# The first layer's 128x256 tile products of five units written as seven block products each, with the work order remade behind them

## The chip, the cores and the metric

The kernel runs on one core of a Trainium2 chip. The metric is device time in microseconds (us) of that core; the median of three runs of the kernel before is 290.37 us (290.33 to 292.88).

## The reference

Two stages follow each other. The first is attention with a mask by hashing: queries and keys of 4 batches, 8 heads, 768 positions and 64 dimensions are projected on six directions, the six signs make a bucket, and a query sees only keys of its own bucket. The second is a two-layer network over the joined heads (512 columns): layer norm, 512 to 2048 columns, relu, back to 512, and the sum with its input.

```
q_bits = (einsum('bhsd,dk->bhsk', q, proj) > 0);  k_bits likewise
mask   = q_bucket[:, :, :, None] == k_bucket[:, :, None, :]
attn   = softmax(where(mask, q @ k.T / sqrt(64), -1e9))
x      = (attn @ v), heads joined            # 4 x 768 x 512
xn     = (x - mean) / sqrt(var + 1e-6) * g_ln
out    = x + relu(xn @ w_ch1) @ w_ch2        # w_ch1: 512 x 2048, w_ch2: 2048 x 512
```

## The kernel before, in words

The work is cut into twelve **units** of 256 query rows, three for each batch, numbered 0 to 11. A unit has two head groups g of four heads. For each unit and group the scores are made in six steps of 128 keys (`S_`, into PSUM tiles `sc`), `E_` takes the exponential on ScalarE (tiles `E`, 128x1024), and `A_` multiplies by the values into the accumulator `acc`. `na` and `nb` normalise into `x`, `nc_` and `ag` make the layer norm's statistics, `ce` the centred and scaled rows `xc`, and `fl` transposes them by a DMA into `xnT`.

The network's first layer is `F_`: eight words per unit, each with eight matmuls of 128 rows of `w_ch1` by 256 moving columns, into a PSUM bank `f`; `R_` (ScalarE or VectorE) takes the relu into `hb`. The second layer of units 1 to 11 is already done by seven block products (`P_`) with sums of `hb` blocks (`ss`) on VectorE and `Y_` adding each product to `x`. `O_` stores.

PSUM is handed out by tag: the tag `pp` has three slots of two banks each (scores and `acc`), the tag `f` has two slots of one bank (everything of the network, and small products). SBUF tiles of many kinds share fifteen slots of tag `E`.

Nothing in the program is scheduled at run time: the string `ORDER` is a list of words like `F.t.7.3` (function, engine, unit, part). The program walks the list and issues each word's instructions to its engine, so each engine's queue is its words in the list's order, and semaphores make an engine wait for what it reads and for slots to come free. `SLOTS` says which slot each tile gets. `WIDE` and `SUMS` are switches; `WIDE` is empty before.

The functions of the seven first-layer products (`w1s`, `bs`, `M_`, `V_`, `U_`, `Q_`, `ru`) stand in the file before as well, but no word of the list before calls them. Their scheme for one unit: `w1s` makes sums of blocks of `w_ch1` (eight instructions for the whole kernel, kept in slots that the loads of queries and keys used, two in `E` slots), `bs` makes four sums of blocks of `xnT`, and `M_` does the seven products in two halves h of 512 hidden columns, each word 8 matmuls with 128 moving columns. Their sums stand in three PSUM tiles per half: `Ma` (products 1, 6, 7, 4), `Mb` (product 2) and `Me` (products 5, 3). `V_` copies a stage of such a sum to SBUF (after products 1, 6 and 5), `U_` adds a PSUM sum and a copy into `hb`, `Q_` takes the relu of the last stage of `Ma`, and `ru` takes the relu of the three blocks that `U_` wrote.

Of the kernel before, what the change touches and what calls it, by code (L numbers as in the profile page):

```python
# [65 lines left out]
tu.v.2.1.0.1 S.t.5.0.0 N.a.5.0.0 S.t.5.0.1 E.a.5.0.0.1 S.t.5.0.2 P.t.2.2 Y.v.2.2 E.a.5.0.0.0 E.a.5.0.0.2  # L66
nb.v.4.0 fl.s.3.1 F.t.3.6 R.v.3.6 ss.v.2.2 P.t.2.1 Y.v.2.1 cv.v.2.0.2 S.t.4.1.3 S.t.4.1.4 N.a.4.1.1 S.t.4.1.5
# [9 lines left out]
R.v.3.1 mr.s.2.1.0 S.t.5.1.3 N.a.5.1.1 S.t.5.1.4 E.a.5.1.1.1 S.t.5.1.5 E.a.5.1.1.2 nb.v.5.0 P.t.3.2 ss.v.3.1
Y.v.3.2 P.t.3.1 P.t.3.5 S.t.6.0.0 E.a.5.1.1.0 CA.v.3.0.1 N.a.6.0.0 mr.s.2.1.1 lv.s.3.0.2 S.t.6.0.1 S.t.6.0.2
E.a.6.0.0.0 E.a.6.0.0.2 ss.v.3.2 Y.v.3.1 ss.v.3.4 Y.v.3.5 P.t.3.6 P.t.3.3 ss.v.3.3 nc.v.5.0 A.t.5.1.0.1
A.t.5.1.0.2 tu.v.3.0.0.2 A.t.5.1.0.0 Y.v.3.6 A.t.5.1.1.0 A.t.5.1.1.2 A.t.5.1.1.1 mr.s.2.1.2 na.v.5.1  # L80
E.a.6.0.0.1 fl.s.4.0 lv.s.2.4.3 P.t.3.7 tu.v.3.0.0.0 Y.v.3.3 nb.v.5.1 O.s.2.3 S.t.6.0.3 N.a.6.0.1 S.t.6.0.4
S.t.6.0.5 CA.a.3.0.0 Y.v.3.7 hm.t.3.0 bt.v.3.0 P.t.3.4 Y.v.3.4 lv.s.3.0.3 F.t.4.6 E.a.6.0.1.0 O.s.2.1
E.a.6.0.1.2 E.a.6.0.1.1 lv.s.3.0.1 nc.v.5.1 ag.v.5.1 ag.v.5.0 R.a.4.6 F.t.4.0 S.t.6.1.0 S.t.6.1.1 N.a.6.1.0
rs.p.5 S.t.6.1.2 R.v.4.0 ce.v.5.0 cv.a.2.4.2 F.t.4.7 E.a.6.1.0.0 cv.v.2.4.0 F.t.4.4 R.a.4.7 ce.v.5.1 on.p.2
fl.s.5.0 A.t.6.0.1.0 A.t.6.0.0.2 tu.v.3.1.0.1 E.a.6.1.0.1 E.a.6.1.0.2 A.t.6.0.1.2 lv.s.3.0.0 R.v.4.4 sp.t.2.0
A.t.6.0.0.1 sc.v.2.0 A.t.6.0.1.1 su.v.2.4 A.t.6.0.0.0 F.t.4.5 F.t.4.2 fl.s.5.1 R.a.4.5 na.v.6.0 nb.v.6.0
F.t.4.1 R.v.4.1 S.t.6.1.3 mw.s.3.0 S.t.6.1.4 N.a.6.1.1 S.t.6.1.5 R.a.4.2 E.a.6.1.1.1 P.t.4.2 O.s.3.0
lv.s.3.4.0 lv.s.3.4.3 tu.v.3.1.0.0 Y.v.4.2 E.a.6.1.1.2 F.t.4.3 tu.v.3.1.1.0 tu.v.3.1.1.2 R.a.4.3 tu.v.3.1.1.1
cv.v.3.0.0 ss.v.4.1 O.s.3.2 F.t.5.3 R.a.5.3 F.t.5.2 R.v.5.2 tu.v.3.1.1.3 E.a.6.1.1.0 P.t.4.1 Y.v.4.1 ss.v.4.2
ss.v.4.4 S.t.7.0.0 N.a.7.0.0 S.t.7.0.1 S.t.7.0.2 E.a.7.0.0.0 E.a.7.0.0.1 P.t.4.5 Y.v.4.5 P.t.4.6 P.t.4.3  # L90
A.t.6.1.0.1 nc.v.6.0 A.t.6.1.1.1 O.s.3.3 Y.v.4.6 A.t.6.1.1.0 Y.v.4.3 sp.t.2.4 sc.a.2.4 A.t.6.1.1.2 A.t.6.1.0.0
# [24 lines left out]
fl.s.8.1 fl.s.8.0 O.s.6.3 N.a.10.0.0 R.v.7.3 R.v.7.1 S.t.10.0.2 P.t.7.2 sp.t.3.4 nb.v.9.0 ss.v.7.1
E.a.10.0.0.1 sc.v.3.4 A.t.9.1.0.0 E.a.10.0.0.0 A.t.9.1.1.0 A.t.9.1.1.1 A.t.9.1.0.1 A.t.9.1.0.2 A.t.9.1.1.2
ss.v.7.3 na.v.9.1 Y.v.7.2 P.t.7.5 E.a.10.0.0.2 S.t.10.1.0 N.a.10.1.0 S.t.10.1.1 E.a.10.1.0.1 S.t.10.1.2
ss.v.7.2 E.a.10.1.0.2 E.a.10.1.0.0 P.t.7.1 Y.v.7.5 ss.v.7.4 P.t.7.3 Y.v.7.1 P.t.7.6 Y.v.7.6 Y.v.7.3 S.t.10.0.3
nb.v.9.1 N.a.10.0.1 S.t.10.0.4 S.t.10.0.5 O.s.6.0 P.t.7.7 Y.v.7.7 E.a.10.0.1.0 O.s.6.2 F.t.8.6 R.a.8.6  # L120
E.a.10.0.1.2 P.t.7.4 F.t.8.7 A.t.10.0.1.0 nc.v.9.0 E.a.10.0.1.1 nc.v.9.1 ag.v.9.1 ag.v.9.0 A.t.10.0.0.1
R.v.8.7 rs.p.9 ce.v.9.0 A.t.10.0.0.0 A.t.10.0.0.2 A.t.10.0.1.2 A.t.10.0.1.1 F.t.8.5 R.a.8.5 ce.v.9.1 Y.v.7.4
F.t.8.0 O.s.7.2 na.v.10.0 R.v.8.0 S.t.10.1.3 fl.s.9.1 S.t.10.1.4 N.a.10.1.1 S.t.10.1.5 O.s.7.0 E.a.10.1.1.1
E.a.10.1.1.2 E.a.10.1.1.0 F.t.8.2 nb.v.10.0 R.v.8.2 F.t.8.3 R.a.8.3 F.t.8.4 R.v.8.4 S.t.11.0.0 N.a.11.0.0
S.t.11.0.1 S.t.11.0.2 F.t.8.1 E.a.11.0.0.0 R.v.8.1 P.t.8.2 O.s.7.3 Y.v.8.2 ss.v.8.1 E.a.11.0.0.2 fl.s.9.0
A.t.10.1.1.0 P.t.8.1 A.t.10.1.0.2 F.t.9.5 Y.v.8.1 A.t.10.1.1.2 A.t.10.1.0.1 A.t.10.1.0.0 A.t.10.1.1.1 ss.v.8.2
ss.v.8.4 R.a.9.5 E.a.11.0.0.1 P.t.8.6 na.v.10.1 nb.v.10.1 P.t.8.5 Y.v.8.5 S.t.11.0.3 ss.v.8.3 Y.v.8.6
# [19 lines left out]

TYPES = "222222333333333333333333"

WIDE = {}  # L150
SUMS = 12

SLOTS = dict(
# [23 lines left out]
def kernel(  # L177
# [751 lines left out]
```

## Time and profile before

The profiled execution took 290.62 us; its span, from the first to the last instruction, is 288.7 us.

| | busy us | share of the span | instructions |
|---|---|---|---|
| TensorE (PE) | 280.6 | 97% | 4588 |
| weight loads (PEld, beside PE) | 226.8 | 79% | 4591 |
| VectorE (DVE) | 223.9 | 78% | 507 |
| ScalarE (ACT) | 201.4 | 70% | 230 |
| GpSimd (POOL) | 27.8 | 10% | 65 |

The granted TensorE clock was 1.0. Busy time is the time in which an engine had an instruction under way; PE's ends are modelled, so the distance from one matmul's start to the next one's start says more than its duration. L-numbers are lines of the kernel: L710 is `F_`, L718 and L720 are `R_` on ScalarE and VectorE, L619 is `A_`, L591 `S_`, L865 `P_`, L870 `Y_`, L850 `ss`.

### The profile page before, as it was taken

How to read it: one execution, taken by the hardware profiler on the slowest of the kernel's cores; microseconds unless marked ns; L12 is line 12 of the kernel's file. 1: busy time of each engine (PE TensorE's matmuls, PEld its weight loads, DVE VectorE, ACT ScalarE, POOL GpSimd, SP SyncE). 2: the span in 40 equal slices, each digit the busy share in tenths (PEclk: the TensorE clock that was granted, in tenths of full speed). 3: DMA queues.
4: the chain of work that ended last, by engine and by line, in shares of the span. 5: the costliest groups of instructions: out<-in, count | busy, mean ns of one | idle time of the engine just before them, and what ended most of it. 6: DMA issues, size and time to landing. Idle time of an engine off the chain costs nothing.

```text
span 288.7 us, 10444 instructions
## 1 busy us (share of the span) xinstructions
PE 280.6 (97%) x4588; PEld 226.8 (79%) x4591; DVE 223.9 (78%) x507; ACT 201.4 (70%) x230; POOL 27.8 (10%) x65
## 2 busy tenths in 40 slices
PE   8999899999999999999999999999999999999994
PEld 4777777558886886887888878888888788898883
DVE  5767899899998998987896687794878486683553
ACT  4889999998786657869767686868685747714140
POOL 4560400110001002001001001000101001010000
PEclk9999999999999999999999999999999999999999
DMA  6999999156912985530710411500040500202162
GB/s 215 366 279 275 211 278 190 54 176 158 319 77 79 171 302 171 138 117 3 186 24 3 102 57 49 114 3 22 2 93 2 111 0 3 39 2 57 26 178 73
DMA packets 31056, 34.11 MB, mean 118 GB/s; under 512 B 15521, under 2 KB 27809, under 8 KB 31010
## 3 DMA queue, kind: packets, MB, share of 16 engines
q1 hardware_dynamic: 25938, 28.72, 34.7%
q0 software_dynamic: 4224, 4.19, 8.8%
q8 instruction: 36, 0.59, 0.8%
q10 hardware_dynamic: 848, 0.53, 0.7%
q14 instruction: 10, 0.08, 0.1%
HBM read 27.86 MB, written 6.88 MB: 120 GB/s over the span
## 4 chain that ended last, share of the span: by engine, by line
PE 92%; DVE 5%; ACT 1%; issue 1%; DVEq 0%; ACTq 0%
PE f L710 29%; PE sc L591 17%; PE X L865 13%; PE acc L619 12%; PE Yb L865 7%; PE Ya L865 3%; PE hp L535 3%; PE hf L403 3%; PE f L813 2%; PE warm L373 1%; DVE T L314 1%; ACT E L608 1%; DVE y L631 1%; DVE st L665 0%; DVE hb L720 0%
## 5 line engine op out<-in xcount | busy, mean ns | idle before, releaser
L608 ACT ACTIVATE E<-sc,bias_sb 128x1024 bf16<-128x1024 f32 x144 | 152.6, 1114 | 38.5 <-PE sc L591 36.8
L710 PE MATMUL f<-xnT,w_sb 128*128 128x256 bf16 x768 | 93.2, 273 | 0.6 <-ACT hb L718 0.2
L710 PEld LDWEIGHTS <-w_sb 128*128 128x128 bf16 x768 | 72.2, 98 | 13.5 <-issue 5.2
L718 ACT ACTIVATE hb<-f 128x512 bf16<-128x512 f32 x60 | 35.6, 598 | 31.8 <-PE f L710 27.7
L591 PE MATMUL sc<-qb,kb 32*128 32x256 bf16 x1152 | 51.4, 267 | 0.0
L591 PE MATMUL sc<-G 6*128 6x256 bf16 (+1 forms) x576 | 42.4, 271 | 0.8 <-ACT E L608 0.8
L619 PE MATMUL acc<-vaug,E 128*128 128x65 bf16 x1152 | 41.5, 193 | 0.2 <-ACT E L608 0.2
L619 PEld LDWEIGHTS <-E 128*128 128x128 bf16 x1152 | 40.1, 97 | 1.9 <-issue 0.6
L865 PEld LDWEIGHTS <-hb 128*128 128x128 bf16 x352 | 33.2, 98 | 7.2 <-issue 3.4
L720 DVE TENSOR_SCALAR hb<-f 128x512 bf16<-128x512 f32 x36 | 24.6, 687 | 16.5 <-PE f L710 16.0
L591 PEld LDWEIGHTS <-kb 32*128 32x128 bf16 x1152 | 30.5, 93 | 1.3
L591 PEld LDWEIGHTS <-G 6*128 6x128 bf16 (+1 forms) x576 | 17.2, 91 | 14.3 <-issue 12.0
L865 PEld LDWEIGHTS <-S 128*128 128x128 bf16 x264 | 24.8, 98 | 4.3 <-issue 1.3
L314 DVE STREAM_TRANSPOSE T<-X 128x384 f32<-128x384 f32 (+2 forms) x52 | 26.1, 536 | 0.0
L631 DVE SCALAR_TENSOR_TENSOR y<-vsB,acc 128x520 f32<-128x520 f32 x24 | 16.5, 689 | 9.8 <-PE acc L619 9.6
L870 DVE TENSOR_TENSOR x<-X,x 128x256 f32<-128x256 f32 x44 | 18.1, 413 | 7.4 <-PE X L865 7.1
L684 POOL TENSOR_SCALAR rs<-mv 128x2 f32<-128x2 f32 x12 | 2.8, 235 | 209.7 <-DVE mv L668 209.6
L865 PE MATMUL Yb<-w_sb,S 128*128 128x256 bf16 x176 | 22.9, 273 | 0.0
L865 PE MATMUL X<-wt,hb 128*128 128x256 bf16 x168 | 21.8, 273 | 0.0
L665 DVE BATCH_NORM_STATS2 st<-x 128x6 f32<-128x256 f32 x48 | 17.6, 412 | 0.3
L641 DVE TENSOR_TENSOR x<-y,rc 128x512 f32<-128x512 f32 x24 | 16.6, 692 | 0.8
L674 DVE TENSOR_SCALAR xc<-x,mv,rs 128x512 bf16<-128x512 f32 x22 | 11.4, 540 | 2.6 <-POOL rs L687 2.5
(94 smaller groups left out, 251.7 us busy)
## 6 DMA issues: line engine op xcount, KB each, us to landing
out_dram<-x SPq DMA_DIRECT2D x45, 128.0 KB
X<-in_k_dram SPq DMA_DIRECT2D x7, 768.0 KB
vn<-in_v_dram SPq DMA_DIRECT2D x24, 192.0 KB
X<-in_q_dram SPq DMA_DIRECT2D x6, 768.0 KB
w_sb<-in_moe_w_ch_dram POOLq DMA_DIRECT2D x8, 512.0 KB, 12.2
vn<-in_v_dram SPq DMA_DIRECT2D x2, 768.0 KB
X<-in_q_dram SPq DMA_DIRECT2D x2, 512.0 KB
Bd<-B SPq DMA_DIRECT2D x6, 96.0 KB
```

The costliest lines, as they stand in the source:

```text
L314: nc.vector.transpose(d[:, j], s[:, j, kj0 : kj0 + n])
L591: m = nc.tensor.matmul(sc(u, g, a, p)[:, bank, 256 * half : 256 * half + 256], lh, rh, start=(rep == 0), stop=(rep == 2), skip_group_check ...
L608: nc.scalar.activation(Ep(u, g, a, p), sc(u, g, a, p), AF.Exp, scale=EXP_SCALE, bias=bias_sb)
L619: nc.tensor.matmul(acc[:, qt, (D + 1) * i : (D + 1) * (i + 1)], Ep(u, g, a, p)[:, bank, 256 * half + P * qt : 256 * half + P * qt + P], va ...
L631: nc.vector.scalar_tensor_tensor(yt(u, g), vs, EPS_ROW, made[f"acc{u}_{g}"][:, :, :A], op0=AOP.mult, op1=AOP.add,)
L641: nc.vector.tensor_tensor(xo, a[:, :, :, 0:D], rc.to_broadcast([P, 2, 4, D]), op=AOP.mult)
L665: nc.vector.bn_stats(stats(u)[:, qt, g], xt(u)[:, qt, 256 * g : 256 * g + 256])
L710: nc.tensor.matmul(f1[:, n].rearrange("p (t x) -> p t x", t=2), w1_sb[:, dt, P * nt : P * nt + P], xnT(u)[:, :, dt], start=(dt == 0), stop ...
L718: nc.scalar.activation(hb(u)[:, 2 * p : 2 * p + 2], f1, AF.Relu)
L720: eng.tensor_scalar_max(hb(u)[:, 2 * p : 2 * p + 2], f1, 0.0)
L865: nc.tensor.matmul(f2, lh[:, n], rh[:, n], start=(first and n == 0), stop=(n == 7), skip_group_check=True)
L870: nc.vector.tensor_tensor(x, made[f"{prod(u, k)}{u}"], x, op=AOP.add)
```

## The change

From unit 5's second score half on the list is written anew (`ORDER` is the same up to there), and the first layer of units 7 to 11 is called as `M`, `V`, `U`, `Q`, `ru` and `bs` words in the place of `F` and `R`. Counted over both lists: 40 `F` words go (320 matmuls with 256 moving columns) and 70 `M` words come (560 with 128). 40 `R` words go (25 on ScalarE, 15 on VectorE). On VectorE come 30 `U`, 10 `V`, 1 `Q`, 9 `ru`, 20 `bs` and 8 `w1s`; on ScalarE 20 `V`, 9 `Q` and 6 `ru`. Two casts of queries or keys (`CA`) move from VectorE to ScalarE, two casts of values (`cv`) the other way. The stores, loads and transposes keep their number; their order on the DMA queue is remade too.

`WIDE` becomes units 10 and 11: their `Ma` and `Me` each take a `pp` slot of their own, of which one bank is used. In units 7, 8 and 9 `Ma`, `Mb` and `Me` share the two `f` slots with everything else that uses them.

```diff
-WIDE = {}
+WIDE = {10,11}
 SLOTS = dict(
...
-    X="0123023120312013",
+    X="012302312031201323",
...
     def Mt(u, name):
         if u in WIDE and name[1] in "ae":
-            both = ps(f"Mae{name[2:]}", [P, 2, 512], "pp")
-            made[name] = both[:, "ae".index(name[1])].rearrange("p (n x) -> p n x", x=P)
-            return made[name]
+            return ps(name, [P, 2, 512], "pp")[:, 0].rearrange("p (n x) -> p n x", x=P)
         return ps(name, [P, 4, P], "f")
...
     def V_(eng, u, p, h):
-        src = made[f"M{'e' if p == 5 else 'a'}{u}{h}"]
+        src = Mt(u, f"M{'e' if p == 5 else 'a'}{u}{h}")
...
     def U_(eng, u, c, h):
         src, other, t, i = {1: ("b", 1, 0, 0), 2: ("e", 6, 1, 0), 4: ("a", 5, 1, 1)}[c]
-        nc.vector.tensor_tensor(hq(u, t, i, h), made[f"M{src}{u}{h}"], made[f"V{u}{other}{h}"], op=AOP.add)
+        nc.vector.tensor_tensor(hq(u, t, i, h), Mt(u, f"M{src}{u}{h}"), made[f"V{u}{other}{h}"], op=AOP.add)
```

(`Q_` changes in the same way; `f`, `pp` and `E` in `SLOTS` are new strings.)

Two lines of the list, the one before and the one after, where unit 8's first layer begins:

```
-F.t.8.0 O.s.7.2 na.v.10.0 R.v.8.0 S.t.10.1.3 fl.s.9.1 S.t.10.1.4 N.a.10.1.1 S.t.10.1.5 O.s.7.0 E.a.10.1.1.1
+V.a.8.6.0 M.t.8.5.0 rs.p.9 S.t.10.1.3 na.v.10.0 nb.v.10.0 nc.v.10.0 N.a.10.1.1 S.t.10.1.4 V.a.8.5.0 M.t.8.7.0
```

**VectorE, unit 8's first layer beside unit 10's normalisation.** In a name the unit comes first, so `hb8` is unit 8's hidden block, `V810` the copy after unit 8's product 1 in half 0, `Ma80` the sum of half 0, `y100`, `rc100` and `x10` unit 10's normalisation, and `xc9` unit 9's centred rows. Before, a piece of the queue reads:

```order
L674 TENSOR_SCALAR xc9_5194<-x9_4925,mv9_5179,rs9_5191 128x512 x2
L870 TENSOR_TENSOR x7_3836<-X7_5046,x7_3836 128x256
L631 SCALAR_TENSOR_TENSOR y100_5250<-vsB3_4087,acc10_0_5163 128x520
L720 TENSOR_SCALAR hb8_5142<-f1_80_5240 128x512
L638 RECIPROCAL rc100_5311<-y100_5250 128x8
L641 TENSOR_TENSOR x10_5313<-y100_5250,rc100_5311 128x2x256
L720 TENSOR_SCALAR hb8_5142<-f1_82_5302 128x512
L720 TENSOR_SCALAR hb8_5142<-f1_84_5326 128x512
L720 TENSOR_SCALAR hb8_5142<-f1_81_5376 128x512
```

Now the same place holds:

```order
L796 COPY V810_5261<-Ma80_5251 128x512
L803 TENSOR_TENSOR hb8_5298<-Mb80_5263,V810_5261 128x4x128
L642 SCALAR_TENSOR_TENSOR y100_5344<-vsB3_3486,acc10_0_5227 128x520
L649 RECIPROCAL rc100_5346<-y100_5344 128x8
L652 TENSOR_TENSOR x10_5348<-y100_5344,rc100_5346 128x2x256
L676 BN_STATS st10_5350<-x10_5348 128x6 x2
L803 TENSOR_TENSOR hb8_5298<-Ma80_5251,V850_5367 128x4x128
L803 TENSOR_TENSOR hb8_5298<-Me80_5318,V860_5316 128x4x128
L685 TENSOR_SCALAR xc9_5399<-x9_4837,mv9_5217,rs9_5327 128x512
L809 TENSOR_SCALAR hb8_5298<-Ma80_5251 128x4x128
L685 TENSOR_SCALAR xc9_5399<-x9_4837,mv9_5217,rs9_5327 128x512
L796 COPY V811_5440<-Ma81_5412 128x512
```

Where four relus stood, each of a finished bank, there now stand copies, sums and one relu of banks that go on being added to; unit 10's normalisation stands between the first sum and the next two, and unit 9's `xc` around `Q` (L809).

**VectorE, the last unit.** `X10`, `Yb10` and `Ya11` are second-layer products of units 10 and 11, `S111` and `S112` the second layer's block sums of unit 11. Before, the last unit's piece begins:

```order
L870 TENSOR_TENSOR x10_5313<-Yb10_6082,x10_5313 128x256
L870 TENSOR_TENSOR x10_5313<-X10_6051,x10_5313 128x256
L850 TENSOR_TENSOR S111_6178<-hb11_6072 128x512
L850 TENSOR_TENSOR hb11_6072<-hb11_6072 128x4x128
L850 TENSOR_TENSOR S112_6181<-S111_6178,hb11_6072 128x512
```

Now:

```order
L803 TENSOR_TENSOR hb11_6407<-Mb111_6482,V1111_6375 128x4x128
L817 TENSOR_SCALAR hb11_6407<-hb11_6407 128x8x128
L879 TENSOR_TENSOR x10_5348<-X10_6377,x10_5348 128x256
L859 TENSOR_TENSOR S111_6503<-hb11_6407 128x512
L803 TENSOR_TENSOR hb11_6407<-Mb110_6514,V1110_6362 128x4x128
L817 TENSOR_SCALAR hb11_6407<-hb11_6407 128x8x128
L859 TENSOR_TENSOR S111_6503<-hb11_6407 128x512
L879 TENSOR_TENSOR x10_5348<-X10_6377,x10_5348 128x256
```

Unit 10's last two additions have moved in between unit 11's first-layer sums, their relus and the first block sums.

More of the change, by code (lines that the diff above doesn't have):

```diff
@@ L77 @@
[L77 to L91, printed above, removed]
@@ new lines @@
+w1s.v.3.1 M.t.7.7.0 A.t.9.0.1.2 w1s.v.4.1 V.a.7.5.0 U.v.7.4.0 M.t.7.3.0 S.t.9.1.3 U.v.7.2.0 A.t.9.0.0.2
+na.v.9.0 M.t.7.4.0 Q.a.7.0 nb.v.9.0 M.t.7.1.1 rs.p.8 S.t.9.1.4 N.a.9.1.1 V.v.7.1.1 E.a.9.1.1.1 M.t.7.2.1
+U.v.7.1.1 S.t.9.1.5 E.a.9.1.1.0 M.t.7.6.1 E.a.9.1.1.2 M.t.7.5.1 ce.v.8.0 S.t.10.0.0 N.a.10.0.0 V.v.7.6.1
+V.v.7.5.1 O.s.6.3 O.s.6.1 M.t.7.7.1 S.t.10.0.2 ru.v.7.1 E.a.10.0.0.0 S.t.10.0.1 E.a.10.0.0.2 U.v.7.4.1
+M.t.7.3.1 nc.v.9.0 M.t.7.4.1 U.v.7.2.1 A.t.9.1.1.2 A.t.9.1.0.0 A.t.9.1.1.0 sp.t.3.4 A.t.9.1.0.2 sc.a.3.4
@@ new lines @@
+A.t.9.1.0.1 A.t.9.1.1.1 ce.v.8.1 fl.s.8.1 Q.a.7.1 E.a.10.0.0.1 ru.v.7.4 P.t.7.1 ru.v.7.2 P.t.7.2 ss.v.7.1
+na.v.9.1 ss.v.7.2 S.t.10.1.0 S.t.10.1.1 O.s.6.2 N.a.10.1.0 S.t.10.1.2 Y.v.7.2 fl.s.8.0 E.a.10.1.0.1
+E.a.10.1.0.2 E.a.10.1.0.0 Y.v.7.1 ss.v.7.4 P.t.7.6 ss.v.7.3 P.t.7.5 Y.v.7.6 P.t.7.7 S.t.10.0.3 N.a.10.0.1
+Y.v.7.5 nb.v.9.1 S.t.10.0.4 nc.v.9.1 E.a.10.0.1.1 O.s.6.0 S.t.10.0.5 Y.v.7.7 P.t.7.3 E.a.10.0.1.0 ag.v.9.0
+P.t.7.4 A.t.10.0.0.0 A.t.10.0.0.2 bs.v.8.3 ag.v.9.1 bs.v.8.1 bs.v.8.2 Y.v.7.3 Y.v.7.4 M.t.8.1.0 bs.v.8.4
@@ L145 @@
+O.a.11.1.1.1 O.s.11.1.0.1 Y.v.11.7.1.0 P.t.11.4 Y.v.11.4 O.a.11.1.1.0 O.s.11.1.0.0
 """
 TYPES = "222222333333333333333333"
-WIDE = {}
+WIDE = {10,11}
 SUMS = 12
```

141 lines of the change are left out of this document (78 added, 63 removed).

## The prediction

> **What bounds the kernel now.** I read the page's busy line first, then the busy time by stretches of the last 175 us, then the waits, then the chain that ended last.
>
> ```profile
> span 288.7 us, 10444 instructions
> PE 280.6 (97%) x4588; PEld 226.8 (79%) x4591; DVE 223.9 (78%) x507; ACT 201.4 (70%) x230; POOL 27.8 (10%) x65
> ```
>
> TensorE is busy for 97% of the span. An average can hide stages, so the second view is the busy time in stretches (columns: length, then busy us and instructions of PE, weight loads, VectorE, ScalarE and GpSimd; granted clock; DMA). 147.4 is where unit 7's scores begin; unit 11's last score half begins at 249.0.
>
> ```profile
> 113.20:147.40 34.20, 34.19 (x574) 28.34 (x575) 30.44 (x66) 27.25 (x32) 1.20 (x4) 1.00 0.39 105
> 147.40:187.40 40.00, 40.00 (x711) 32.88 (x714) 30.45 (x66) 29.27 (x33) 2.13 (x6) 1.00 0.24 59
> 187.40:208.30 20.90, 20.90 (x361) 17.69 (x360) 15.33 (x33) 14.95 (x17) 0.93 (x2) 1.00 0.04 9
> 208.30:228.50 20.20, 20.20 (x356) 17.03 (x356) 14.82 (x33) 13.72 (x16) 0.93 (x2) 1.00 0.30 67
> 228.50:249.00 20.50, 20.50 (x333) 17.71 (x332) 13.45 (x29) 12.74 (x16) 0.93 (x2) 1.00 0.11 22
> 249.00:288.70 39.70, 35.38 (x381) 31.09 (x380) 21.98 (x52) 12.09 (x18) 0.93 (x2) 1.00 0.23 61
> ```
>
> From 113 us to the last matmul TensorE has no hole. VectorE is busy 89% in the first of these stretches and 65 to 76% after it. The waits say the same: the two engines that empty the first layer's banks wait for TensorE, for long, and no such time stands against TensorE.
>
> ```profile
> ACT hb L718 <- PE f L710: 27.7, 27, 4.7
> DVE hb L720 <- PE f L710: 16.0, 17, 4.8
> ```
>
> So a microsecond of matmul saved after 147 us is worth a microsecond, as long as VectorE and ScalarE stay out of TensorE's way. Both halves of that sentence have to be priced.
>
> **TensorE: what the products save.** The chain of waits (start, length, what) gives the spacing of matmuls with their weight loads.
>
> ```profile
> 236.48 1.10 PE sc L591 x36
> 252.06 1.47 PE acc L619 x48
> 258.76 6.13 PE f L710 x56
> ```
>
> A first-layer matmul with 256 moving columns takes 6.13/56 = 109.5 ns; a value matmul with 65 columns, which also loads a new 128x128 block each time, takes 1.47/48 = 30.6 ns. No row has 128 columns with a new block. The straight line through both gives 30.6 + 63 x (109.5 - 30.6)/191 = 56.6 ns. Bounds: half of the 256-column row, 54.7 ns, and the 65-column row scaled, 60.3 ns. Removed are 320 x 109.5 ns = 35.0 us, added 560 x 56.6 ns = 31.7 us. **TensorE saves 3.3 us** (1.3 to 4.4). Every other matmul stays.
>
> **VectorE and ScalarE: what it costs.** Groups of instructions by line and shape (busy us, mean ns, then idle time ahead and its releaser):
>
> ```profile
> L608 ACT ACTIVATE E<-sc,bias_sb 128x1024 bf16<-128x1024 f32 x144 | 152.6, 1114 | 38.5 <-PE sc L591 36.8 <-DVE S L850 1.1 <-ACT E L608 0.3
> L718 ACT ACTIVATE hb<-f 128x512 bf16<-128x512 f32 x60 | 35.6, 598 | 31.8 <-PE f L710 27.7 <-PE sc L591 3.9
> L720 DVE TENSOR_SCALAR hb<-f 128x512 bf16<-128x512 f32 x36 | 24.6, 687 | 16.5 <-PE f L710 16.0
> L641 DVE TENSOR_TENSOR x<-y,rc 128x512 f32<-128x512 f32 x24 | 16.6, 692 | 0.8
> L850 DVE TENSOR_TENSOR S<-hb 128x1024 bf16<-128x1024 bf16 x10 | 6.9, 687 | 0.6 <-ACT hb L718 0.3
> L850 DVE TENSOR_TENSOR S<-hb 128x512 bf16<-128x512 bf16 x2 | 0.8, 424 | 4.6 <-ACT hb L718 4.6
> L464 DVE TENSOR_SCALAR w_sb<-w_sb,gT 128x512 bf16<-128x512 bf16 x12 | 3.4, 346 | 0.0
> L325 DVE CAST kb<-T 128x1536 bf16<-128x1536 f32 x5 | 4.7, 937 | 0.0
> L321 ACT ACTIVATE qb<-T 128x1536 bf16<-128x1536 f32 x2 | 3.0, 1483 | 1.7 <-PE sc L591 1.6
> L483 ACT CAST vaug<-vn 128x768 bf16<-128x768 f32 x7 | 5.8, 829 | 0.3 <-PE sc L591 0.3
> L485 DVE CAST vaug<-vn 128x768 bf16<-128x768 f32 x6 | 3.2, 534 | 0.0
> ```
>
> VectorE loses 15 relus (10.3 us) and two casts of 937 ns (1.9). It gains 30 sums `U` of 512 columns at the 692 ns of the two-operand row (20.8), 10 copies and one relu out of PSUM at 687 ns (7.6), 8 weight sums at 687 ns (5.5), 20 sums `bs` of 256 columns, for which the rows of 1024 and 512 columns (687 and 424 ns) leave 293 ns (5.9), 9 `ru` of 1024 columns between the 346 ns of the one-operand row of half the length and 687 ns, taken at 500 ns (4.5; 3.1 to 6.2), and two casts of 534 ns (1.1). That is **33 us more**. ScalarE loses 25 relus (15.0) and two casts of 829 ns (1.7) and gains 29 `V` and `Q` of 512 columns at 598 ns (17.3), 6 `ru` at the 1114 ns of the 1024-column row (6.7) and two casts of 1483 ns (3.0): 10 us more.
>
> Nearly all of it falls after 147.4 us. There VectorE had 96.0 us of work by the table of stretches; with 33 it has 129, in 137.1 - 3.3 = 134 us up to the last matmul (its row started at 283.6 and lasted 0.9). That is 96%. Back-to-back rows overlap a little: the relu below lasts 0.67 us and the next row starts 0.60 us after it, so the true need is between 118 us (half of some 280 rows gain 0.08) and 129 us, 88 to 96%. ScalarE has 82.8 + 10 = 93 us, 69%, and is not the bound.
>
> ```profile
> 241.12 0.67 DVE L720 TENSOR_SCALAR hb<-f 128x512 bf16<-128x512 f32 x1
> 241.72 0.27 DVE L668 BATCH_NORM_AGGREGATE mv<-st 128x2 f32<-128x12 f32 x2
> ```
>
> **The new waits.** Before, a bank was filled by eight matmuls in 0.87 us and emptied once. Now a bank is read in between: product 1, copy, product 6, copy, product 7, sum, product 4, relu, and the next product cannot be added until the reader is done. The reader starts 0.20 us after the product's last matmul has started through (product `X` ends where `Yc` starts at 283.44, its addition starts at 283.64), and TensorE follows a VectorE row 0.05 us later (266.74 to 266.79).
>
> ```profile
> 283.44 1.04 PE L865 MATMUL Yc<-wt,hb 128*128 128x256 bf16 x8
> 283.64 0.75 DVE L870 TENSOR_TENSOR x<-X,x 128x256 f32<-128x256 f32 x2 [0.45 <-PE X L865]
> 266.40 0.34 DVE x L870
> 266.75 0.04 issue
> 266.79 1.03 PE f L710 x8
> ```
>
> So a step costs 0.45 us of product and 0.20 + 0.69 + 0.05 = 0.94 us of turn-round. From product 1's start to product 4's end that is 4 x 0.45 + 3 x 0.94 = 4.6 us. In unit 8's first half TensorE has in the same time its seven products (3.15), four `A` words of 8 x 30.6 ns (1.0) and three `S` words (a third of 1.10 each): 5.2 us. The turn-rounds would hide, with 0.6 us to spare, if VectorE came at once. But its queue there (the order shown above) is, start to start, a copy and a sum (0.65 and 0.60), unit 10's normalisation and statistics (0.73, 0.85 and 0.70), two sums (1.2) and one `xc` (0.5), together 5.2 us, as much as TensorE has. Taken one after the other, product 4 waits 0.24 us for the sum behind the statistics, the next half's product 1 waits 0.15 us for its bank, and product 2 waits 0.28 us for `Q`, which stands behind an `xc`: **0.7 us in 9.3 us**.
>
> ```profile
> L631 DVE SCALAR_TENSOR_TENSOR y<-vsB,acc 128x520 f32<-128x520 f32 x24 | 16.5, 689 | 9.8 <-PE acc L619 9.6
> L638 DVE RECIPROCAL rc<-y 128x8 f32<-128x8 f32 x24 | 4.7, 196 | 0.4
> L665 DVE BATCH_NORM_STATS2 st<-x 128x6 f32<-128x256 f32 x48 | 17.6, 412 | 0.3
> L674 DVE TENSOR_SCALAR xc<-x,mv,rs 128x512 bf16<-128x512 f32 x22 | 11.4, 540 | 2.6 <-POOL rs L687 2.5
> ```
>
> Per half the wait lies between nothing (the stretch at 113 us has VectorE at 89% and TensorE without a hole) and 0.7 us. I take 0.5 us for the six halves of units 7 to 9, whose sums fill both `f` banks, and none for the four of units 10 and 11, whose `Ma` and `Me` lie in `pp`: 3.0 us (0 to 7 over all ten halves).
>
> The end itself I cost at nothing: product 2 of unit 11's second layer needs the bank that the last `U` frees, 0.20 + 0.69 + 0.05 = 0.94 us after the last `Mb`, and ahead of it TensorE still has a first-layer product (0.45) and unit 10's last second-layer product (0.87). If that cover is gone, the end is 0.9 us later. The weight sums run before VectorE is full and the changed load order moves transfers in a stretch with DMA at 0.04 to 0.39; both cost nothing.
>
> Sum, against the profiled execution of 290.6 us: -3.3 + 3.0 = -0.3, so 290.3 us; the median of the runs is 0.25 us under the profiled one, so **290.0 us**.
>
> **A rule against it.** The weight loads are busy 79%, and each of the 560 products brings one. The Trainium skill, "TensorE: Matmul & The Clock Gate", section "Back-to-back issue gap", says that pairs of load and matmul sustain about 81 ns at 128 columns. By that rule 560 products cost 45.4 us and the kernel would lose 10.4 us instead of winning 3.3; an estimate from that page. This case's trace disagrees where it can: 30.6 ns for a pair with 65 columns.
>
> **Rivals.** *The waits stay hidden.* For it: 170 us without a hole before, with VectorE once at 89%. Then only TensorE's saving counts: 290.4 - 3.3 = 287.1 us (286.0 with 4.4). Against: VectorE at up to 96%. Chance 0.25. *VectorE becomes the bound.* From a wait of 0.33 us per half on, the change loses; with 0.7 in all ten halves it is +3.7, 294.1 us, and with VectorE idle a little at the end besides, 296. For it: unit 8's queue, which is full without any margin. Against: ScalarE has a third of its time free and takes two thirds of the copies. Chance 0.25. *Loads are not hidden at 128 columns.* If a pair cost what a load row lasts, 98 ns, 560 would cost 54.9 us: +19.9, 310 us. Only the 30.6 ns speak on it, and against it. Chance 0.03. *The product price is no saving*: at 60.3 ns only 1.3 us are won, and with 3.0 us of waits it is 292.1, inside my own case.
>
> **How the numbers follow.** A measurement of this kernel tells about 1% from no change, that is 287.5 and 293.3 us. My case, saving and waits cancelling within that, has 0.47; its own range is 287.5 to 293.3. Faster by over 1%: 0.25. Slower by over 1%: 0.25 + 0.03 = 0.28. The range reaches from near the hidden-waits case to VectorE as the bound: 286.6 to 294.8.
>
> **What would show it.** Right: `M` words at 0.45 us in the chain; VectorE busy at about 257 us in all (223.9 + 33) and 90% or more after 150 us; waits of TensorE on `V`, `U` or `Q` of some tenths in units 7 to 9, 3 us together; the last matmul within 1 us of 284.5. Wrong: `M` words above 0.48 us; TensorE without a hole (then 287); TensorE's waits over 5 us, or waits on ScalarE's `V` behind exponentials.

## The result, and the profile after

The changed kernel takes 289.44 us (median of 20 runs), the kernel before 290.87 us (20 runs): a ratio of 0.9954 with a 95% interval of 0.9941 to 0.9967, which is 1.3 us less (1.0 to 1.7). The prediction had said 290.0 us in a range of 286.6 to 294.8, and no change beyond 1% as the likeliest case. The profiled execution took 289.45 us, its span is 287.7 us (before 290.62 and 288.7).

The page of the changed kernel, span and busy time:

```profile
span 287.7 us, 11038 instructions
PE 279.4 (97%) x4831; PEld 227.3 (79%) x4831; DVE 249.3 (87%) x570; ACT 210.7 (73%) x240; POOL 27.9 (10%) x65
```

TensorE's busy time fell by 1.2 us, VectorE's rose by 25.4 us and ScalarE's by 9.3. The stretches of the changed kernel (length, then busy us and instructions of PE, weight loads, VectorE, ScalarE and GpSimd; granted clock; DMA share) show where VectorE's work went:

```profile
147.40:187.40 40.00, 40.00 (x690) 32.77 (x678) 34.56 (x77) 31.56 (x36) 2.07 (x4) 1.00 0.30 72
187.40:208.30 20.90, 20.68 (x406) 17.31 (x404) 19.00 (x40) 14.72 (x16) 0.93 (x2) 1.00 0.06 15
208.30:228.50 20.20, 20.20 (x401) 17.02 (x402) 18.77 (x44) 14.54 (x16) 0.92 (x2) 1.00 0.13 28
228.50:249.00 20.50, 20.40 (x420) 18.11 (x413) 17.84 (x42) 16.36 (x18) 0.93 (x2) 1.00 0.31 67
249.00:283.30 34.30, 34.30 (x457) 31.72 (x454) 31.77 (x75) 14.78 (x24) 0.92 (x2) 1.00 0.18 44
```

VectorE is busy 86% at first, where it had been 76%, and 87 to 93% in the four stretches from 187 us on, where it had been 73, 73, 66 and, up to the last matmul, 61%. TensorE shows its first holes: 0.22 us between 187 and 208 us, 0.10 between 228 and 249. (Busy time can hide short waits, because a matmul's modelled end reaches past the next one's start; the starts below say more.)

The chain of waits of the changed kernel gives the price of a product, and the row of the last second-layer product its end:

```profile
254.45 1.34 PE Ma L785 x24
```

```profile
282.26 1.04 PE L874 MATMUL Yc<-wt,hb 128*128 128x256 bf16 x8
```

A pair of load and matmul with 128 columns takes 1.34/24 = 55.8 ns. The last second-layer product starts at 282.26 us, before at 283.44: TensorE is done 1.2 us earlier. (The two lists part a little earlier than at unit 5's second score half, right behind its first three score words, which start at 97.75 us before and at 97.73 now. So the 1.2 us are not there already ahead of the change.)

**Two ways in which the saving is given back.** By the prices of the traces the products save 320 x 109.5 - 560 x 55.8 ns = 35.0 - 31.2 = 3.8 us. Of these 1.2 arrived; 2.6 us are missing. TensorE's rows of before and after around a block of scores show the first loss. Before (start, length, matmuls, how many):

```profile
203.46 1.03 PE L710 MATMUL f<-xnT,w_sb 128*128 128x256 bf16 x8
204.42 0.29 PE L591 MATMUL sc<-G 6*128 6x256 bf16 x4
...
204.76 0.28 PE L591 MATMUL sc<-G 6*128 6x256 bf16 x4
...
205.10 0.28 PE L591 MATMUL sc<-G 6*128 6x256 bf16 x4
...
205.53 1.70 PE L710 MATMUL f<-xnT,w_sb 128*128 128x256 bf16 x14
```

The eight `F` matmuls ahead of the block take 204.42 - 203.46 = 0.96 us instead of 8 x 109.5 ns = 0.87: 0.1 us is lost on the way into the score matmuls, which use 6 and 32 rows of the array. The three score words start 0.34 us apart, but from the last one's start at 205.10 to the next `F` it is 0.43: 0.1 us on the way out. Before, the scores come as whole blocks of three words. After, at the same place:

```profile
202.81 0.29 PE L602 MATMUL sc<-G 6*128 6x256 bf16 x4
...
204.50 0.29 PE L602 MATMUL sc<-G 6*128 6x256 bf16 x4
...
204.94 0.62 PE L785 MATMUL Mb<-xnT,w_sb 128*128 128x128 bf16 x8
205.49 0.29 PE L602 MATMUL sc<-G 6*128 6x256 bf16 x4
...
206.02 0.61 PE L785 MATMUL Ma<-bs,Wx 128*128 128x128 bf16 x8
206.82 0.61 PE L785 MATMUL Me<-bs,Wx 128*128 128x128 bf16 x8 [0.19 <-DVE hb L803]
```

One block of three score words (unit 9's last) has been cut into three single ones, with products between. A lone score word takes 0.44 us to the next start (204.50 to 204.94) where one inside a block takes 0.34, and the product ahead of one takes 0.55 (204.94 to 205.49) where a product takes 0.45. From unit 7's first scores to the last matmul there are 26 blocks of scores where there were 20; six more at about 0.21 us make 1.3 us. (Five blocks are cut, this one twice. Four of them are cut by first-layer products, one of unit 7 by a second-layer product.)

The second loss is the one the prediction was about: the product at 206.02 should take 0.45 us and the next starts 0.80 us after it, 0.35 us late, for a sum on VectorE. Such waits, between 0.02 and 0.35 us each, add up to some 1.1 to 1.3 us beyond those of before. Nearly all of them lie between 200 and 236 us, in units 7 and 8; one of 0.26 us stands ahead of a second-layer product of unit 8. From 236 to 276 us no start is more than 0.1 us late except at the edges of score blocks.

The waits of the changed kernel, where the two engines that empty the banks still wait for TensorE's first layer (units 0 to 6), VectorE for 5.7 us where it had been 16.0 (over 21 such rows in the place of 36):

```profile
ACT hb L729 <- PE f L721: 6.1, 8, 2.3
DVE hb L731 <- PE f L721: 5.7, 11, 1.1
```

### The profile page after: what moved, and what is told of

The parts are those of the page before. It is cut to its first block, busy times and chain, and to the rows that moved or that the text cites. A ratio compares the mean times of both kernels' runs of the same rounds, so it can differ in the third digit from the quotient of the medians.

```text
span 287.7 us, 11038 instructions
## 1 busy us (share of the span) xinstructions
PE 279.4 (97%) x4831; PEld 227.3 (79%) x4831; DVE 249.3 (87%) x570; ACT 210.7 (73%) x240; POOL 27.9 (10%) x65
## 4 chain that ended last, share of the span: by engine, by line
PE 90%; DVE 7%; ACT 1%; issue 1%; DVEq 0%; ACTq 0%
PE sc L602 17%; PE f L721 16%; PE X L874 13%; PE acc L630 12%; PE Yb L874 7%; PE Ma L785 6%; PE Ya L874 3%; PE Me L785 3%; PE hp L546 3%; PE hf L414 3%; PE f L822 2%; PE Mb L785 1%; PE warm L384 1%; DVE y L642 1%; DVE T L325 1%; DVE x L652 1%
## 5 line engine op out<-in xcount | busy, mean ns | idle before, releaser
L619 ACT ACTIVATE E<-sc,bias_sb 128x1024 bf16<-128x1024 f32 x144 | 151.8, 1112 | 31.2 <-PE sc L602 29.5
L721 PE MATMUL f<-xnT,w_sb 128*128 128x256 bf16 x448 | 55.4, 273 | 0.4 <-ACT hb L729 0.2
L602 PE MATMUL sc<-qb,kb 32*128 32x256 bf16 x1152 | 52.0, 267 | 0.0
L721 PEld LDWEIGHTS <-w_sb 128*128 128x128 bf16 x448 | 41.6, 98 | 8.8 <-issue 4.0
L630 PE MATMUL acc<-vaug,E 128*128 128x65 bf16 x1152 | 42.9, 194 | 0.2 <-ACT E L619 0.2
L630 PEld LDWEIGHTS <-E 128*128 128x128 bf16 x1152 | 40.7, 97 | 2.0 <-issue 0.8
L874 PEld LDWEIGHTS <-hb 128*128 128x128 bf16 x352 | 32.6, 98 | 6.9 <-issue 2.9
L729 ACT ACTIVATE hb<-f 128x512 bf16<-128x512 f32 x35 | 20.8, 598 | 9.5 <-PE f L721 6.1
L731 DVE TENSOR_SCALAR hb<-f 128x512 bf16<-128x512 f32 x21 | 14.3, 689 | 5.8 <-PE f L721 5.7
L785 PEld LDWEIGHTS <-Wx 128*128 128x128 bf16 x240 | 14.6, 97 | 1.4 <-issue 1.2
```

The lines of the kernel that those rows point to most:

```text
L602: m = nc.tensor.matmul(sc(u, g, a, p)[:, bank, 256 * half : 256 * half + 256], lh, rh, start=(rep == 0), stop=(rep == 2), skip_group_check ...
L619: nc.scalar.activation(Ep(u, g, a, p), sc(u, g, a, p), AF.Exp, scale=EXP_SCALE, bias=bias_sb)
L630: nc.tensor.matmul(acc[:, qt, (D + 1) * i : (D + 1) * (i + 1)], Ep(u, g, a, p)[:, bank, 256 * half + P * qt : 256 * half + P * qt + P], va ...
L721: nc.tensor.matmul(f1[:, n].rearrange("p (t x) -> p t x", t=2), w1_sb[:, dt, P * nt : P * nt + P], xnT(u)[:, :, dt], start=(dt == 0), stop ...
L729: nc.scalar.activation(hb(u)[:, 2 * p : 2 * p + 2], f1, AF.Relu)
L785: nc.tensor.matmul(m[:, n], lh(kt)[:, P * nt : P * nt + P], rh[:, kt], start=(first and n == 0 and kt == 0), stop=(kt == 1), skip_group_ch ...
```

## The experiments

Theory 1: the products save 3.8 us; 1.3 us are lost at the edges of six more score blocks and about as much in waits for VectorE. Rivals were that edges cost nothing, that VectorE's load is the whole loss, or that the order of its words is.

**Score blocks of before, cut (first way).** Ten blocks were cut by moving the matmul word ahead of a block behind the block's first score word; no work was added. One of the ten:

```diff
-P.t.6.2 Y.v.6.2 fl.s.7.0 su.v.3.4 S.t.9.0.0 S.t.9.0.1
+fl.s.7.0 su.v.3.4 S.t.9.0.0 P.t.6.2 Y.v.6.2 S.t.9.0.1
```

> The kernel before, with one word moved: ten blocks of three score words (units 8 to 10) are each broken by the matmul word that stood in front of them, so that this word runs after the first score word. Nothing is added or left out. Theory 1 (TensorE pays about 0.1 us each time it goes into or out of a score block): ten more breaks of 0.2 us, +2.0 us over the kernel before. Rival (breaks cost nothing; the time that the change gave back is VectorE's fullness): within 0.4 us of before.

Measured: 295.16 us, ratio 1.0133 (1.0104 to 1.0163), 3.9 us more. That is almost twice the expected loss, and the trace shows one reason: the first score word was brought forward, and now waits for the exponential that frees its PSUM slot. TensorE's rows of this kernel:

```profile
172.89 0.28 PE L589 MATMUL sc<-G 6*128 6x256 bf16 x2
173.59 0.28 PE L589 MATMUL sc<-G 6*128 6x256 bf16 x2 [0.42 <-ACT E L606]
173.60 0.49 PE L589 MATMUL sc<-qb,kb 32*128 32x256 bf16 x8
```

So the run mixes two costs and doesn't tell edges from slots.

**Score blocks of before, cut (second way).** The matmul word that follows a block was put ahead of the block's last score word instead, so that no score word comes earlier:

```diff
-S.t.10.0.2 P.t.7.2
+P.t.7.2 S.t.10.0.2
```

> Before, with ten score blocks of three words broken in two: the first- or second-layer word that follows the block is put ahead of the block's last score word, so that the scores ahead of it are not advanced and need no earlier slot. No work is added or left out. Theory 1 (TensorE pays about 0.10 us on its way into a run of score matmuls and 0.11 us on its way out): ten more of each, +2.1 us, 1.8 to 2.9 with some delayed exponentials; the trace shows 0.1 us at each edge and few waits. Rival (a break by itself is free, and what the earlier run with broken blocks lost was waits for slots): +0.5 us or less.

Measured: 295.08 us, ratio 1.0136 (1.0095 to 1.0177). This number needs a correction: the granted clock of the profiled execution was 0.94 between 30 and 60 us, long before the first changed word, and 1.0 around it,

```profile
30.00:60.00 30.00, 28.78 (x560) 20.53 (x563) 25.96 (x64) 27.28 (x32) 5.11 (x10) 0.94 0.77 169
```

so I count from a block ahead of the cuts, which starts at 169.96 here and at 168.08 in the kernel before, to the last product, at 288.75 here and 283.44 there: 118.8 against 115.4 us, 3.4 us more, above the 1.8 to 2.9 that had been expected. TensorE's rows of one cut block:

```profile
190.80 1.05 PE L708 MATMUL f<-xnT,w_sb 128*128 128x256 bf16 x8
191.78 0.29 PE L589 MATMUL sc<-G 6*128 6x256 bf16 x4
...
192.22 1.05 PE L708 MATMUL f<-xnT,w_sb 128*128 128x256 bf16 x8
```

The `F` word between two score words takes 0.98 us instead of 0.87, and a lone score word 0.44 (191.78 to 192.22) instead of 0.34. The trace has these two prices, 0.10 or 0.11 us each, at nearly every one of the ten cuts: 2.1 us of the 3.4. The rest, 1.3 us, goes to waits behind the cut blocks, whose last exponentials now come later; the largest are like this one, 0.4 us behind the `F` word:

```profile
193.51 0.41 PE L617 MATMUL acc<-vaug,E 128*128 128x65 bf16 x8 [0.24 <-ACT E L606]
```

The rival, that a cut by itself is free, falls.

**The score blocks of the change, put together again.** Four of its five cut blocks were made whole, five of the six breaks. One of the moves:

```diff
-V.a.8.5.0 M.t.8.7.0 ... U.v.8.4.0 U.v.8.2.0 S.t.10.1.5
+S.t.10.1.5 V.a.8.5.0 M.t.8.7.0 ... U.v.8.4.0 U.v.8.2.0
```

> The changed kernel with the score blocks of units 9, 10 and 11 that its products break put together again (five breaks fewer), all other words in their order. Theory 1: the breaks are worth 5 x 0.2 = 1.0 us, but the score words also filled time in which TensorE waits for copies and sums, so some of it comes back as waits: 0 to 1.0 us faster than the changed kernel, 288.4 to 289.4 us. Rival (VectorE is the bound): no difference, as VectorE's queue is the same.

Measured: 291.16 us, ratio 1.0015 (0.9990 to 1.0041), about 1.8 us more than the change as it is. Neither expectation came true. The edges are gone and waits stand in their place. TensorE's rows of this kernel, where the change has its three single score words:

```profile
205.56 0.61 PE L783 MATMUL Ma<-bs,Wx 128*128 128x128 bf16 x8
206.44 0.61 PE L783 MATMUL Me<-bs,Wx 128*128 128x128 bf16 x8 [0.27 <-DVE hb L801]
206.98 0.36 PE L600 MATMUL sc<-G 6*128 6x256 bf16 x4
...
208.06 0.29 PE L600 MATMUL sc<-G 6*128 6x256 bf16 x4 [0.50 <-ACT E L617]
```

Product 5 is 0.43 us late, the second score word 0.7 us (0.34 would follow the first), three later products 0.5 to 0.6. So these cuts are the price of covering the turn-rounds: five of them cost about 1.0 us, and without them the kernel is slower.

**VectorE relieved.** All `ru` words were left out, and the layer norm's statistics of units 7 to 11 read a quarter of their columns, so the relu of the three summed blocks and three quarters of the statistics are missing from this kernel:

```diff
+        n = 64 if u > 6 else 256
         for qt in range(2):
-            nc.vector.bn_stats(stats(u)[:, qt, g], xt(u)[:, qt, 256 * g : 256 * g + 256])
+            nc.vector.bn_stats(stats(u)[:, qt, g], xt(u)[:, qt, 256 * g : 256 * g + n])
```

> The changed kernel with less work on VectorE: the relu of the blocks that the sums wrote is left out (nine times 0.42 us on VectorE, six times 1.06 us on ScalarE), and units 7 to 11 take their layer norm statistics over a quarter of the columns (20 instructions, about 0.2 us shorter each), in all some 7.8 us off VectorE. Theory 1 (TensorE's waits in units 7 to 9 are about 1.4 us in all, the rest is breaks of score blocks): 0.3 to 1.2 us faster than the changed kernel. Rival (VectorE is the bound of the last 90 us): 4 us faster or more, until TensorE's own 3.8 us are all won.

Measured: 289.25 us, ratio 0.9929 (0.9902 to 0.9956), 0.7 us less than the change (the intervals of the two overlap). In the traces, from a word ahead of the first one left out (109.86 us in the change, 110.23 here) to the last second-layer product (282.26, here 282.24), it is 0.4 us less. The wait of 0.35 us that the change has behind 206.02 is still there, as long as it was (0.80 from start to start):

```profile
206.38 0.61 PE L783 MATMUL Ma<-bs,Wx 128*128 128x128 bf16 x8
207.18 0.61 PE L783 MATMUL Me<-bs,Wx 128*128 128x128 bf16 x8 [0.19 <-DVE hb L801]
```

With it, the waits in the first layer of units 7 and 8 come to 1.2 us, as in the change; the 0.26 us ahead of unit 8's second-layer product are gone. So the first layer's waits did not shrink with VectorE's total; what counts for them seems to be what stands ahead of a copy or sum in the queue; the run with another order, below, shows it for one of them.

**VectorE loaded.** Ahead of VectorE's first copy or sum of each half of units 7 to 11 it makes two sums that nobody reads:

```diff
+    def bal(eng, u, h):
+        b = sb("ballast", [P, 512], BF16, "bl", 1)
+        for i in range(2):
+            eng.tensor_tensor(b, w1_sb[:, 0, 512 * i : 512 * i + 512], w1_sb[:, 1, 512 * i : 512 * i + 512], op=AOP.add)
```

> The changed kernel with 0.75 us of idle work on VectorE ahead of the first copy or sum of each of the ten product halves (two sums of 512 columns of the first layer's weights into a tile that nobody reads), 7.5 us in all. Theory 1 (VectorE has some tenths of slack in each half, and each wait opens where its queue is full): +2 to +4.5 us over the changed kernel. Rival (VectorE is the bound): +6 to +7.5 us. If VectorE does not matter at all: under +0.7 us.

Measured: 295.52 us, ratio 1.0155 (1.0119 to 1.0190), 5.8 us more than the change, above the 2 to 4.5 us of theory 1 and just under the 6 to 7.5 of the rival. The busy lines of both, first the relieved kernel, then the loaded one:

```profile
PE 279.4 (97%) x4828; PEld 227.5 (79%) x4831; DVE 244.2 (85%) x561; ACT 205.1 (71%) x234; POOL 27.8 (10%) x65
```

```profile
PE 280.3 (96%) x4828; PEld 227.4 (78%) x4831; DVE 256.9 (88%) x590; ACT 210.7 (72%) x240; POOL 28.4 (10%) x65
```

5.1 us less on VectorE (and 5.6 less on ScalarE) bring 0.7 us; 7.6 us more on VectorE cost 5.8. Three quarters of the time added at these places go over into TensorE's time. But the two runs differ in place as well as in sign: the added sums stand right ahead of the copies and sums that TensorE waits for, the work left out mostly does not. How much is VectorE's total and how much the place was not separated. In the loaded kernel the product that starts at 206.02 in the change waits for the copy of product 1:

```profile
206.22 0.39 PE L601 MATMUL sc<-qb,kb 32*128 32x256 bf16 x8
207.43 0.61 PE L784 MATMUL Ma<-bs,Wx 128*128 128x128 bf16 x8 [0.82 <-DVE V L800]
```

**Another order on VectorE.** Words that nobody waits for soon (an `nb` of unit 9 and one of unit 10, an `nc` of unit 10, three `ce`) were moved behind those that TensorE waits for, and one `U` with its `ru` forward, for instance:

```diff
-nb.v.9.0 M.t.7.1.1 ... V.v.7.1.1 ... U.v.7.1.1
+M.t.7.1.1 ... V.v.7.1.1 ... U.v.7.1.1 nb.v.9.0
```

> The changed kernel with nine words moved on VectorE in units 7 to 10 (and what follows from them on the DMA queue): unit 9's and 10's normalisation, statistics and centring stand behind the copies and sums that TensorE waits for, not ahead of them. No work is added or left out, TensorE's queue is the same. Theory 1 (1.0 us of TensorE's waits in units 7 and 8 are places in VectorE's queue): 0.4 to 1.0 us faster than the changed kernel, 288.4 to 289.0 us. Rival (VectorE's total is the bound): no difference.

Measured: 290.71 us, ratio 0.9993 (0.9973 to 1.0013), 1.1 us more than the change; 0.4 to 1.0 us less had been expected, and no difference by the rival. The rows of this kernel:

```profile
205.99 0.62 PE L783 MATMUL Ma<-bs,Wx 128*128 128x128 bf16 x8
206.45 0.61 PE L783 MATMUL Me<-bs,Wx 128*128 128x128 bf16 x8
206.99 0.64 PE L600 MATMUL sc<-G 6*128 6x256 bf16 x4
...
236.11 1.04 PE L872 MATMUL Yb<-w_sb,S 128*128 128x256 bf16 x8
237.82 1.03 PE L872 MATMUL X<-wt,S 128*128 128x256 bf16 x8 [0.68 <-DVE x L877]
```

The 0.35 us ahead of product 5 are gone (206.45 follows 205.99 after 0.46): with unit 9's `nb` out of its way the copy of product 1 comes earlier. So that wait was a matter of order. But other waits have opened. The next score word is stretched (0.64 us for a row that takes 0.29), and the largest is in unit 8's second layer: `X` starts 1.71 us after `Yb`, which takes 0.87. That is 0.84 us late, where the change loses 0.32 at the same two products, for an addition on VectorE that now stands behind unit 10's `nb`, moved to this place. So this order is no better: what is moved back is waited for at its new place. Whether another order would keep the 0.35 us without the 0.84 was not tried.

**Products in the last two units alone.** If edges and VectorE's load in units 7 to 9 take the saving, products in units 10 and 11 alone, on the order of before, should keep theirs: 128 x 109.2 - 224 x 55.7 ns = 1.5 us, with whole score blocks, and VectorE's load is lower by three units' sums. Four versions of the list behind the last score word were run.

> The seven products in units 10 and 11 only: the list of the kernel before up to unit 11's last score word (with the eight weight sums put into VectorE's waits), then products of units 10 and 11 between the second-layer products, as in the changed kernel. No product meets a score block. TensorE's work is 128 matmuls of 109 ns less and 224 of 55.7 ns more than before: -1.5 us. Theory 1 (products among score words of units 7 and 8 pay their saving back in breaks and waits, products after the last score block do not): 1.0 to 1.5 us faster than before, as fast as the changed kernel with two fifths of its products. Rival (VectorE's fullness is the price, each unit's products cost it the same): two fifths of the changed kernel's 1.3 us, 0.5 us faster than before.

First version: 291.19 us, ratio 1.0009 (0.9984 to 1.0035), no gain. The largest of the waits, at unit 11's first product:

```profile
264.00 0.61 PE L777 MATMUL Ma<-bs,w_sb 128*128 128x128 bf16 x8
265.71 0.62 PE L777 MATMUL Ma<-xnT,w_sb 128*128 128x128 bf16 x8 [1.10 <-DMA xnT<-xc]
```

Unit 11's rows, centred too late on VectorE, come 1.26 us late out of their transposes. The second version brings them forward:

```diff
-P.t.9.5 Y.v.9.5 bs.v.10.3 bs.v.10.4 nc.v.11.1 ... U.v.10.4.0 ... U.v.10.2.0 ce.v.11.1 ... ce.v.11.0
+nc.v.11.1 ag.v.11.0 ag.v.11.1 rs.p.11 bs.v.10.3 bs.v.10.4 Y.v.9.5 ... ce.v.11.1 ce.v.11.0 ... U.v.10.4.0 U.v.10.2.0
```

> Products in units 10 and 11 only, on the order of before, as in the run of the same kind before it; new in this one: the normalisation of unit 11 goes ahead of five other VectorE words so that its transposed rows land some 1.5 us earlier, and a product 2 stands between product 7 and product 3 of unit 10's second half. Theory 1 (a product pair costs 55.7 ns wherever it stands, and what is lost is lost to named waits): 16 F words go (128 x 109.2 ns = 14.0 us) and 28 M words come (224 x 55.7 ns = 12.5 us), the score blocks stay whole; with the 1.26 and 0.44 us waits gone and some 0.5 us of small ones left the time is 1.0 us under before (0.6 to 1.5), the last matmul starts at 282.2 to 282.9. Rival (without score and value matmuls beside them the seven products always wait for their copies and sums): the waits come up elsewhere in the last 25 us, 1.5 us of them or more, and the time is that of before within 0.4 us.

290.56 us, ratio 0.9991 (0.9968 to 1.0013): inconclusive. The wait for the transposes was gone, and the next product waited in its place:

```profile
264.82 0.61 PE L777 MATMUL Ma<-xnT,w_sb 128*128 128x128 bf16 x8
266.24 0.62 PE L777 MATMUL Me<-bs,Wx 128*128 128x128 bf16 x8 [0.81 <-DVE bs L755]
```

The view names the block sum `bs`. The third version has it ahead of unit 10's last `U`, and ScalarE makes three copies earlier or in VectorE's place:

```diff
-U.v.10.1.1 M.t.10.3.1 U.v.10.2.1 ru.v.10.2 M.t.10.4.1 Q.a.10.1 bs.v.11.1
+U.v.10.1.1 ru.v.10.1 M.t.10.3.1 bs.v.11.1 U.v.10.2.1 ru.a.10.4 M.t.10.4.1 Q.a.10.1
```

> Products in units 10 and 11 only, a third time: the run of the same kind before it still lost 0.97 us at the product after unit 11's first one, whose block sum stood on VectorE behind three first-layer sums and a relu, and 0.27 us at unit 10's last product, behind a copy that ScalarE made after a relu. Now that block sum stands ahead of unit 10's last first-layer sum, the relu of unit 10's first block ahead of it too, ScalarE makes the two copies before the relu, and the copy after unit 11's product 5 goes to ScalarE. Theory 1 (what is lost is lost to named waits, and these stood in the order of VectorE's words): the time is 0.8 to 1.4 us under before, no wait over 0.3 us after 250 us. Rival (turn-rounds of the products in the last units cannot be hidden, whatever the order): the waits open at the following products, and the time stays within 0.4 us of before.

290.14 us, ratio 0.9988 (0.9963 to 1.0013), again no gain that can be told:

```profile
266.12 0.61 PE L777 MATMUL Me<-bs,Wx 128*128 128x128 bf16 x8 [0.81 <-DVE hb L795]
```

The wait is as long as it was, and now the view names the sum into `hb`. The product needs a PSUM slot too, the one that unit 10's last `U` frees; of the two things it waited for, the view had named the one that came last. The fourth version moves that `U` forward (and ScalarE's last `Q` ahead of a relu):

```diff
-U.v.10.1.1 ru.v.10.1 M.t.10.3.1 bs.v.11.1 U.v.10.2.1 ... M.t.10.4.1 Q.a.10.1 M.t.11.1.1
+M.t.10.3.1 U.v.10.2.1 bs.v.11.1 U.v.10.1.1 M.t.11.1.1 M.t.10.4.1 Q.a.10.1
```

> Products in units 10 and 11 only, once more: in the run before it unit 11's product 5 still waited 0.81 us, not for a block sum but for its PSUM slot, which unit 10's last first-layer sum frees, and unit 10's last product 0.28 us for a first-layer sum. Now that sum stands two VectorE words earlier, unit 11's first product goes ahead of unit 10's last one, and ScalarE takes the last relu of the bank ahead of the relu of two blocks. Theory 1 (the saving of 1.5 us is there as soon as no named wait eats it): 0.7 to 1.4 us under before, the last matmul starts before 283.0, no wait over 0.3 us after 250 us. Rival (the products of the last units hand any time saved to the next wait): within 0.4 us of before.

289.96 us, ratio 0.9976 (0.9954 to 0.9998), 0.7 us less than before. Its rows at the same product and at the end:

```profile
264.67 0.62 PE L777 MATMUL Me<-bs,Wx 128*128 128x128 bf16 x8
...
282.32 1.04 PE L866 MATMUL Yc<-wt,hb 128*128 128x256 bf16 x8
```

The last second-layer product starts 1.1 us earlier than before; 0.1 us of it stands in the trace already ahead of the first changed matmul, so 1.0 us comes out of 1.5 saved (0.3 in the second and third versions, none in the first). Theory 1 holds for the last two units, and most of what was missing in the other versions were the waits named. Two units bring 0.7 us (0.1 to 1.3), all five 1.3 us (1.0 to 1.7); this version doesn't beat the change, whose three other units add little, if anything that can be told from these intervals. That fits the sum: units 7 to 9 save 192 x 109.5 - 336 x 55.8 ns = 2.3 us, and the six edges and the waits of units 7 and 8 take 2.4 to 2.6.

## Why the prediction was right, point by point

**The product's price.** 56.6 ns had been worked out from the rows of 256 and 65 columns; 55.8 ns were measured. 560 products cost 31.2 us, so the saving was 3.8 us in the place of 3.3, within the bounds given (1.3 to 4.4). The rule that spoke against the change, 81 ns by the Trainium skill, "TensorE: Matmul & The Clock Gate", section "Back-to-back issue gap", does not hold here: by it these 24 matmuls would have taken 1.94 us, the row has 1.34. The rivals of unhidden loads (98 ns) and of a dearer product (60.3 ns) fall with the same row.

**VectorE's load.** 33 us more were predicted as a sum of durations; in the traces the durations add up to 31.7 us more, the busy time to 25.4. The terms were right or a little high. Groups by line, with mean ns:

```profile
L803 DVE TENSOR_TENSOR hb<-Ma,V 128x512 bf16<-128x512 f32 x10 | 6.8, 686 | 0.7 <-PE Ma L785 0.5
L817 DVE TENSOR_SCALAR hb<-hb 128x1024 bf16<-128x1024 bf16 x9 | 3.7, 423 | 0.1
L763 DVE TENSOR_TENSOR bs<-xnT 128x256 bf16<-128x256 bf16 x10 | 2.7, 275 | 0.0
```

`U` took 686 ns (692 predicted), `ru` 423 (500), `bs` 275 (293): together 1.2 us less. The rest is overlap, which the prediction had named for the need but not taken off the 257 us that it gave as a sign: rows that follow each other start 0.60 us apart and last 0.69, and busy time counts the common part once.

```profile
207.13 0.69 DVE L796 COPY V<-Ma 128x512 f32<-128x512 f32 x1
207.73 0.68 DVE L796 COPY V<-Me 128x512 f32<-128x512 f32 x1
```

So the sum of durations was right and the sign of 257 us was not; nor was "90% or more after 150 us" met everywhere: VectorE is at 86% up to 187 us and at 87 to 93% from there on. (Of the kernel before, the prediction reads 65 to 76% after 147 us; the last stretch of its table, 21.98 in 39.70 us, is 55%, or 61% up to the last matmul.)

**The waits.** 3.0 us were predicted, 0.5 us for each half of units 7 to 9 and none in 10 and 11. The traces show 1.1 to 1.3 us. The kind is right, a product that waits for what stands in VectorE's queue, and so are units 7 and 8 and the absence from 10 and 11; against the prediction, unit 9 has none to speak of. The walk through unit 8's first half had 0.24 us ahead of product 4, 0.15 ahead of the next half's product 1 and 0.28 at its product 2, 0.67 in all. Measured are 0.07, 0.14 and 0.12:

```profile
225.94 0.61 PE L785 MATMUL Ma<-bs,w_sb 128*128 128x128 bf16 x8
226.53 0.61 PE L785 MATMUL Ma<-xnT,w_sb 128*128 128x128 bf16 x8
...
227.63 0.62 PE L785 MATMUL Mb<-xnT,w_sb 128*128 128x128 bf16 x8
```

(0.59 from 225.94 to 226.53 where a product takes 0.45; the score word that starts at 227.07 gives way at 227.63, 0.12 later than a lone one.) A walk that takes every row at its start-to-start time in a queue without slack comes out twice too long. The end, costed at nothing, cost little: the first second-layer product of unit 11 waits for nothing, and two later ones are 0.1 us late each.

**What was missing.** The sum had no term for the cut score blocks, 1.3 us: the diff of the list showed single score words between the products, and every block of before has its 0.1 us on either side in the trace. Beside it stands a rule of the Trainium skill, "TensorEngine Tiling (Array Packing)", section "Key Properties": a change of the tiling mode drains the array. The trace fits it: where nothing is waited for, runs of 128-row matmuls follow each other without loss, and the ways to and from the 6- and 32-row score matmuls cost, 0.21 us together for a lone word. That it is a drain, no run here shows; that a cut costs, the second way of cutting shows.

So the sum should have read -3.8 + 1.3 + 1.2 = -1.3 where it read -3.3 + 3.0 = -0.3. The time came out within 0.6 us, and that is in part luck. A wait taken too long (3.0 for 1.2) stood in for an edge not seen (1.3) and a saving taken 0.5 too small; the change in time was still 1.0 us off. Half of that vanished because the kernel before, 290.37 us over three runs when the prediction was made, has 290.87 over 20. Of the four signs given for a right prediction only the first came as stated, the product word at 0.45 us; VectorE's 257 us, the 3 us of waits and a last matmul within 1 us of 284.5 (it ended at 283.3) did not. The rival of hidden waits (287.1) was too low by what edges and waits took, and the one with VectorE as the bound (294 to 296) is where the kernel came with 7.6 us more on VectorE (295.5).

## What to carry to other kernels

Price every term of a trade on TensorE from starts to starts, and count how often the new order switches between small-row and full-row matmuls: an edge that costs a tenth of a microsecond decides a change that saves three. When work moves to an engine that is at 90%, load and relieve that engine by a known amount, and follow one wait through all the runs: here 0.35 us stayed when 5 us of VectorE's work were left out, and went when one word was moved out of the way. Then look at who waits at the new place of what was moved. When a wait is removed and the next product waits as long, look for a second thing that it needed all along, here a PSUM slot behind a block sum.

## What the hardware showed that was not expected

The ways into and out of a run of score matmuls cost 0.09 to 0.11 us each, whether the run is one word or three, and whether the neighbours are first-layer, second-layer or product matmuls. A pair of load and matmul with 128 columns runs at 55.8 ns while loads, 98 ns each, are busy 79% of the span. And VectorE's time goes over into TensorE's unevenly: 5 us under the change's load bring 0.7 us, 7.6 us over it, put right ahead of what TensorE waits for, cost 5.8.
